# Last layer's first product as seven block products instead of eight, in a fused attention and two-layer kernel on one Trainium2 core

## Chip, core and metric

One NeuronCore of one Trainium2 chip runs the whole program. The metric is device microseconds for one execution, lower is better. All matrix products are done in fp32r with each operand split into a high and a low part, three matmuls (high·high, high·low, low·high) for each product.

## What is computed

```python
attn_out = _attn_ref(q, k, v, s)              # 4 x 8 heads x 576 tokens x 64, causal, decay bias
x = attn_out.transpose(0, 2, 1, 3).reshape(2304, 512)
a, b = x @ w_a, x @ w_b                       # 512 -> 1536, twice
y = (a * b) @ w_out                           # 1536 -> 512
h = y @ w_in2                                 # 512 -> 2048: the last layer's first product
g = np.maximum(h, 0.0) ** 2
out = g @ w_out2                              # 2048 -> 512: the last layer's second product
```

The weights come as 64-bit floats and are decoded on the chip to fp32 (helper `decode`), then split into high and low.

## The kernel before

A planner (`Plan`) takes every operation in program order with a stream ("first", "att", "moe", "next", "late"), a cost and the buffers it needs, and lists the instructions of each engine in one static order: the earliest start by its own cost figures, and among those that can start, the lowest rank (`Plan.RANK`, then program order). A DMA is issued on SP only, and SP's order is part of that list, so a DMA whose wait is not over holds up every DMA behind it. All instructions are recorded at line 246, so the profile is read by tile names.

The work, in order of time: attention of the four batches with the middle layer's chunks (`moe1`, tiles `ab`, `py`) interleaved; after the attention's pools are closed (`swap`, about 460 us) only the middle layer's last chunks of 448 tokens run; from about 723 us the last layer.

The middle layer keeps the high parts of its weights in 36 buffers "wh" and fetches the low parts for every chunk from DRAM (`lo<-wlab`, 512 KB; `loo<-wlo`, 384 KB). TensorE (PE) accumulates into three PSUM banks of the pool "mm" (`mm_bank`).

The last layer before: `split2(f)` decodes for each of the 16 blocks of 128 hidden features a block of w_in2 and one of w_out2 into `w2h`, `w2l`, kept in SBUF in buffers that the middle layer frees (tag "wh", stream "late"). The loop over `t0` takes 512 tokens at a time (four and a half times); `load_y` brings their four 128-row blocks of y from DRAM and splits them (`yhy`/`yly` or `xhy`/`xly`, double-buffered). For each f, 12 matmuls of 512 columns fill one bank `ph` (4 blocks of the contraction, 3 passes); ScalarE (ACT) and VectorE (DVE) form relu(h)² and its split, `g2h`/`g2l`; `second(f)` of the f before adds 4 × 3 matmuls of 512 columns into the four banks `po`, which are evicted and stored after the last f:

```python
for d in range(ND):
    h_, l_ = yy(d, 0, n)
    pairs += [(w2h[f, 0][:, d, :], h_), (w2h[f, 0][:, d, :], l_), (w2l[f, 0][:, d, :], h_)]
matmul(ps, n, pairs)
...
if prev is not None:
    second(*prev)
```

Of the kernel before, what the change touches and what calls it, by code (L numbers as in the profile page):

```python
# [7 lines left out]
F32 = mybir.dt.float32  # L8
F32R = mybir.dt.float32r
# [239 lines left out]
def attention_moe_moe(tc, q, k, v, s, w_a, w_b, w_out, w_in2, w_out2, out):  # L249
# [14 lines left out]
    NT1 = 2  # L264
    CC = 448
    W = 512
    NLATE = 11
    EARLY = 10
    AHEAD = 6
    LAG = 0.0  # L270
    LF = 5
    MORE = 12
# [25 lines left out]
    def gated(name, shape, dtype, tag, bufs, nm):  # L298
        return pl.tile(pool(name), shape, dtype, tag, bufs, nm, swapped)
# [11 lines left out]
        return pl.tile(pool("mm"), [P, 512], F32, "mm", 3, name)  # L311


    def pe(cost, calls, out, ins):
        pl.add({"PE": (cost, calls, False)}, [out], ins)

    def matmul(out, n, pairs, passes=1.0):
        calls = [
            ("matmul", (out, a, b), {"start": i == 0, "stop": i == len(pairs) - 1}) for i, (a, b) in enumerate(pairs)
        ]  # L320
        cost = len(pairs) * (passes * max(n, 256 if passes == 1 else n) / 2.4 + 13)
        pe(cost, calls, out, [x for pair in pairs for x in pair])
# [389 lines left out]
    def attention(b):  # L712
# [30 lines left out]
            unit(p)  # L743
        return steps

    def new_x(nm, second=False):
        if second:
            ts = [gated("lop", [P, ND, W], F32R, t, 1, f"{t}{nm}") for t in ("yh", "yl")]
# [10 lines left out]
        subtract(n, xl, xl.bitcast(F32), xh.bitcast(F32))  # L759


    def decode(w, by_col, f, hi, lo, nm, raw, t, takes, by):
# [7 lines left out]
        dma(raw.rearrange("p (d c) -> p d c", d=ND), src, 512, takes)  # L770
        words = raw.rearrange("p (n w) -> p n w", w=2)
        low, high = words[:, :, 0], words[:, :, 1]
        hi, lo = (x.rearrange("p d c -> p (d c)") for x in (hi, lo))
# [12 lines left out]
        gps("tensor_tensor", n, out=t, in0=t, in1=low, op=ALU.add)  # L786
        copy(n, hi, t.bitcast(F32), by="A")
        subtract(n, lo, t.bitcast(F32), hi.bitcast(F32), by=by)

# [7 lines left out]
    def split_w(f):  # L797
        def g():
# [5 lines left out]
            for i, w in enumerate((w_a, w_b, w_out)):  # L804
                hi = sb([P, ND, P], F32R, "wh", 3 * NF1, f"wh{f}_{i}")
                if i < 2:
                    lo = ab[:, i].part(i) if ab else spare(i)
                else:
                    lo = spare(i) if f < LF1 else sb([P, ND, P], F32R, "lo1", 1, f"wlo{f}")
                k_ = 3 * f + i  # L810
                t = ts[k_ % 2]
                if f < 9:
                    t = sb([P, DM], I32, "wh", 3 * NF1, f"wt{f}_{i}") if i == 2 else ts[i]
                words = [*raws, *more] if k_ < MORE else raws
                decode(w, i < 2, f, hi, lo, f"w{f}_{i}", words[k_ % len(words)], t, (), "PD")
# [139 lines left out]
    pl.stream = "moe"  # L955


    w2h, w2l = {}, {}
    spare = []

    def split2(f):
        for i in range(2):
            hi = sb([P, ND, P], F32R, "wh", 3 * NF1, f"w2h{f}_{i}")
            n = 2 * NF2 - 2 * f - i
            if n > NLATE:
                lo = gated("lop", [P, ND, P], F32R, "w2l", 2 * NF2 - NLATE, f"w2l{f}_{i}")
            elif n > 4:
                wide, tag, bufs = {
                    5: (W, "gh", GB), 6: (W, "gl", GB), 7: (2 * GRP * P, "loo", 2), 8: (2 * GRP * P, "loo", 2),
                    9: (DM, "lo1", 1), 10: (W, f"y{ND - 1}", 1),  # L970
                    11: (W, f"y{ND - 2}", 1),
                }[n]
                lo = sb([P, wide], F32R, tag, bufs, f"w2l{f}_{i}")[:, :DM].rearrange("p (d c) -> p d c", c=P)
            else:
                if n % 2 == 0:
                    spare.append(sb([P, 2, ND, P], F32R, "lo", 3, f"w2l{f}"))
                lo = spare[-1][:, i].part(i)
            nm = f"v{f}_{i}"
            raw = gated("lop", [P, 2 * DM], I32, "tmp", 3, f"{nm}r")
            t = sb([P, DM], I32, "wh", 3 * NF1, f"{nm}t")  # L980
            decode(w_in2 if i == 0 else w_out2, i == 0, f, hi, lo, nm, raw, t, (t, hi, lo), "P")
            w2h[f, i], w2l[f, i] = hi, lo

    y_tokens = {}

    def load_y(t0):
        n = min(512, NT - t0)
        yy = y_tokens[t0] = new_x(f"y{t0}", t0 % 1024 == 0)
        for d in range(ND):
            pieces = []  # L990
            for c, (g0, g1) in enumerate(spans):
                l, r = max(t0, g0), min(t0 + n, g1)
                if l < r:
                    pieces.append((l - t0, r - l, yd[c][d][:, l - g0 : r - g0].part(d)))
            split_x(yy, d, 0, n, pieces)

    load_y(0)
    pl.stream = "late"
    for f in range(EARLY):
        split2(f)  # L1000
    pl.stream = "moe"
    for t0 in range(0, NT, 512):
        n = min(512, NT - t0)
        yy = y_tokens.pop(t0)
        nt = n // P
        po = [gated("po", [P, 512], F32, "po", 4, f"po{t0}_{i}") for i in range(nt)]
        prev = None

        def second(f, gh, gl):
            wo, wl = (t[f, 1].rearrange("p d c -> p (d c)") for t in (w2h, w2l))  # L1010
            for i in range(nt):
                at_ = slice(i * P, i * P + P)
                calls = [
                    ("matmul", (po[i], a[:, at_], w), {"start": f == 0 and z == 0, "stop": f == NF2 - 1 and z == 2})
                    for z, (a, w) in enumerate(((gh, wo), (gh, wl), (gl, wo)))
                ]
                pe(3 * 216, calls, po[i], [gh, gl, wo, wl])

        for f in range(NF2):
            if f == AHEAD and t0 + 512 < NT:  # L1020
                load_y(t0 + 512)
            ps = mm_bank(f"ph{t0}_{f}")[:, :n]
            pairs = []
            for d in range(ND):
                h_, l_ = yy(d, 0, n)
                pairs += [(w2h[f, 0][:, d, :], h_), (w2h[f, 0][:, d, :], l_), (w2l[f, 0][:, d, :], h_)]
            matmul(ps, n, pairs)
            r = sb([P, 512], F32, "a", 2, f"r{t0}_{f}")[:, :n]
            act("activation", n, r, ps, AF.Relu, psum=True)
            dve("scalar_tensor_tensor", n, ps, ps, 0.0, r, op0=ALU.max, op1=ALU.mult)  # L1030
            gh = sb([P, W], F32R, "gh", GB, f"g2h{t0}_{f}")
            gl = sb([P, W], F32R, "gl", GB, f"g2l{t0}_{f}")
            act("copy", n, gh[:, :n], ps, psum=True)
            dve("tensor_tensor", n, out=gl[:, :n], in0=ps, in1=gh[:, :n].bitcast(F32), op=ALU.subtract)
# [5 lines left out]
            prev = (f, gh, gl)  # L1040
            if t0 == 0 and f < NF2 - EARLY:
                pl.stream = "late"
                split2(EARLY + f)
                pl.stream = "moe"
        second(*prev)
        for i in range(nt):
# [42 lines left out]
```

## Time and profile before

| | |
|---|---|
| time, median of 3 runs | 1128.77 us (1125.85 to 1129.11) |
| profiled execution, first to last instruction (span) | 1128.5 us; no other time of that execution is recorded |
| PE (matmul) busy | 1099.6 us, 97% |
| DVE, ACT, POOL busy | 625.6, 482.9, 318.4 us |
| DMA | 132.10 MB, mean 117 GB/s; HBM read 99.54 MB, written 22.69 MB |
| granted TensorE clock | 1.0 from 300 us to 1100 us |

The granted clock 1.0 is the higher of TensorE's two levels, 2.4 GHz. A row of a timeline gives start, duration, engine, operation and tile; matmuls overlap, so what one costs is the distance between starts. A row of the chain of waits merges matmuls of one tile that follow each other.

### The profile page before, as it was taken

The page shows a single profiled execution, that of the slowest core. Times are in us where ns is not written, and L with a number is a line of the kernel's source. Part 1 is how long each engine was busy: PE and PEld are TensorE (multiplying, and loading weights), DVE is VectorE, ACT ScalarE, POOL GpSimd, SP SyncE. Part 2 cuts the span into 40 slices and gives each one's busy share as a digit, 9 for nine tenths or more (in the row PEclk, how much of TensorE's full clock was granted, in tenths as well). Part 3 has the DMA queues.
Part 4 walks back from the last instruction along what each step waited for, and adds up shares of the span by engine and source line. Part 5 has one row for each costly group of instructions (what it writes and reads, how often), then busy time and mean ns, then how long its engine had stood idle before and what let it go on. Part 6 is the DMA issues. An engine that isn't in the chain of part 4 may idle for free.

```text
span 1128.5 us, 15440 instructions
## 1 busy us (share of the span) xinstructions
PE 1099.6 (97%) x5488; PEld 928.5 (82%) x5488; DVE 625.6 (55%) x1174; ACT 482.9 (43%) x1121; POOL 318.4 (28%) x274
## 2 busy tenths in 40 slices
PE   5998999999999999999999999999999999999998
PEld 3665777778899999899999999888888888888887
DVE  5776797878777777723222358987232232232232
ACT  4545686667666665421121244445232222232222
POOL 2434655655433333200100147766010010000000
PEclk9977899999999999999999999999999999999999
DMA  6433467666544443443433677642110010010010
GB/s 206 153 110 105 142 194 229 187 207 194 151 148 130 135 143 103 143 147 116 164 108 116 186 246 234 195 147 75 38 38 1 21 54 1 1 57 1 1 38 19
DMA packets 83692, 132.10 MB, mean 117 GB/s; under 512 B 9104, under 2 KB 53648, under 8 KB 83616
## 3 DMA queue, kind: packets, MB, share of 16 engines
q1 hardware_dynamic: 83616, 131.12, 37.1%
q8 instruction: 43, 0.70, 0.3%
q14 instruction: 33, 0.27, 0.1%
HBM read 99.54 MB, written 22.69 MB: 108 GB/s over the span
## 4 chain that ended last, share of the span: by engine, by line
PE 90%; DVE 6%; DMA 2%; issue 1%; SPq 0%; ACT 0%; POOL 0%; DVEq 0%; ACTq 0%; POOLq 0%
PE ab L246 24%; PE ph L246 17%; PE po L246 17%; PE py L246 12%; PE av L246 7%; PE st L246 7%; PE pt L246 5%; DVE e L246 1%; DMA roomxh<-in_moe_w_a 1%; SPq L246 0%; DVE neg L246 0%; DMA v_0r<-in_moe_w_in 0%; DVE v_1t L246 0%; DMA v_1r<-in_moe_w_out 0%; DVE v_0t L246 0%
## 5 line engine op out<-in xcount | busy, mean ns | idle before, releaser
L246 DVE SCALAR_TENSOR_TENSOR ph<-ph,r 128x512 f32<-128x512 f32 (+1 forms) x80 | 51.6, 645 | 195.0 <-ACT r L246 195.0
L246 ACT ACTIVATE r<-ph 128x512 f32<-128x512 f32 (+1 forms) x80 | 44.5, 556 | 212.5 <-PE ph L246 212.5
L246 PE MATMUL po<-w2h,g2h 128*128 128x512 f32 x288 | 112.4, 390 | 0.0
L246 PE MATMUL po<-w2h,g2l 128*128 128x512 f32 x288 | 112.3, 390 | 0.0
L246 PE MATMUL po<-w2l,g2h 128*128 128x512 f32 x288 | 112.3, 390 | 0.0
L246 ACT ACTIVATE e<-st,neg 128x192 f32<-128x192 f32 (+2 forms) x192 | 91.1, 479 | 46.8 <-DVE neg L246 42.9
L246 PE MATMUL ab<-xh,wh 128*128 128x448 f32 x288 | 106.3, 369 | 0.0
L246 PE MATMUL ab<-xh,lo 128*128 128x448 f32 x288 | 105.3, 365 | 0.0
L246 PE MATMUL ab<-xl,wh 128*128 128x448 f32 x288 | 105.2, 365 | 0.0
L246 DVE TENSOR_TENSOR ab<-ab,a 128x448 f32<-128x448 f32 (+1 forms) x60 | 38.6, 644 | 105.1 <-PE ab L246 102.5
L246 PE MATMUL pt<-ident,e 128*128 128x128 f32 (+2 forms) x480 | 86.0, 290 | 10.9 <-DVE e L246 9.0
L246 DVE TENSOR_REDUCE neg<-st 128x1 f32<-128x192 f32 (+2 forms) x192 | 77.6, 425 | 27.9 <-PE st L246 19.8
L246 PE MATMUL py<-gh,wh 128*128 128x448 f32 (+1 forms) x240 | 90.8, 379 | 0.5 <-DVE gl L246 0.5
L246 PE MATMUL py<-gh,loo 128*128 128x448 f32 (+1 forms) x240 | 89.0, 371 | 0.0
L246 PE MATMUL py<-gl,wh 128*128 128x448 f32 (+1 forms) x240 | 88.9, 370 | 0.0
L246 PEld LDWEIGHTS pt<-ident,e 128*128 128x128 f32 (+2 forms) x480 | 55.7, 138 | 37.2 <-issue 11.7
L246 PE MATMUL av<-ph,val 128*128 128x256 f32 (+3 forms) x256 | 81.5, 409 | 3.1 <-DVE ph L246 1.4
L246 DVE TENSOR_TENSOR g2l<-ph,g2h 128x512 fp32r<-128x512 f32 (+1 forms) x80 | 51.0, 637 | 41.8 <-ACT g2h L246 37.2
L246 ACT COPY a<-ab 128x448 f32<-128x448 f32 (+1 forms) x60 | 32.6, 544 | 91.6 <-PE ab L246 91.5
L246 PE MATMUL ph<-yhy,w2h 128*128 128x512 f32 (+1 forms) x192 | 67.9, 354 | 0.4 <-DVE gl L246 0.4
L246 PE MATMUL ph<-yhy,w2l 128*128 128x512 f32 (+1 forms) x192 | 67.9, 354 | 0.0
L246 PE MATMUL ph<-yly,w2h 128*128 128x512 f32 (+1 forms) x192 | 67.9, 354 | 0.0
(205 smaller groups left out, 2640.2 us busy)
## 6 DMA issues: line engine op xcount, KB each, us to landing
lo<-wlab SPq DMA_DIRECT2D x48, 512.0 KB
loo<-wlo SPq DMA_DIRECT2D x40, 384.0 KB
v_0r<-in_moe_w_in SPq DMA_DIRECT2D x16, 512.0 KB
v_1r<-in_moe_w_out SPq DMA_DIRECT2D x16, 512.0 KB
roomxh<-in_moe_w_a SPq DMA_DIRECT2D x10, 512.0 KB
roomxh<-in_moe_w_b SPq DMA_DIRECT2D x10, 512.0 KB
roomxl<-in_moe_w_out SPq DMA_DIRECT2D x9, 512.0 KB
out<-o SPq DMA_DIRECT2D x18, 256.0 KB
```

Of the source, the lines that this page charges most:

```text
L246: getattr(eng, method)(*map(real, args), **{k: real(a) for k, a in kw.items()})
```

## The change

The 2 × 2 block form of Strassen's product (Winograd's variant, seven products). A pair `j` of feature blocks (f = 2j, 2j+1) is the one dimension of two, the upper and lower 256 of the 512 contraction rows the second, and two neighbouring groups of 384 tokens the third. Tokens go in sets of 768 (three sets).

- `split_in(j)` (stream "late", before `load_y(0)`) decodes the two blocks of w_in2, forms the four sums of weight blocks (`combine`), splits seven blocks of 128 × 256 into high and low (`w2h`, `w2l`, 1792 columns each) and writes both to DRAM (`w2q`, 917,504 bytes each).
- For each pair and token set two DMAs bring these back (`w`, tag "wq", 4 buffers, so two pairs).
- `load_y(t0)` brings four blocks of 128 × 768, forms four sums in place and splits seven blocks (`b11`, `b22`, `b21`, `t1` to `t4`, each high and low: 14 buffers "yq", all in use by one token set).
- A pair is seven products of 6 matmuls of 384 columns. Products with `start=False` add to a bank that ACT has already read: bank a takes b11, then t2, t3, t4; a second bank b21; a third t1, then b22. Such a product has to wait for the ACT copy (`kept`: s1, s2, s3) or the DVE sum (`relu2`) that reads the bank.
- `second(j, g)` takes both feature blocks and six token groups: 6 × 6 matmuls of 512 columns. The sixth `po` bank is one of the three "mm" banks.
- w_out2 is decoded as before (`split_out`, 16 blocks kept in SBUF).

```diff
+    def split_in(j):
+        t = temp(I32, f"w2t{j}")
+        ts = [t[:, i * DM : i * DM + DM].part(i) for i in range(2)]
         for i in range(2):
...
+            words(w_in2, True, 2 * j + i, temp(I32, f"w2r{j}_{i}"), ts[i])
+        f0, f1 = (x.bitcast(F32) for x in ts)
+        a11, a12, a21, a22 = f0[:, :QW], f0[:, QW:], f1[:, :QW], f1[:, QW:]
+        hi, lo = block(f"w2h{j}"), block(f"w2l{j}")
...
+        split(0, 2, 0, f0)
+        split(2, 3, 1, a22)
+        combine(QW, a22, a21, a22, ALU.add)
+        combine(QW, a21, a11, a21)
+        combine(QW, a11, a22, a11)
+        combine(QW, a12, a12, a11)
+        split(3, 7, 2, t.bitcast(F32))
+        for z, x in enumerate((hi, lo)):
+            dma(w2q[j][z], x.rearrange("p q c -> p (q c)").bitcast(F32), 1200)
...
+        for j in range(PAIRS):
+            nm = f"{t0}_{j}"
+            w = [block(f"w{nm}_{z}") for z in range(2)]
+            for z in range(2):
+                dma(w[z].rearrange("p q c -> p (q c)").bitcast(F32), w2q[j][z], 896)
+
+            def product(ps, q, x, start=True):
+                xh, xl = yq[x]
+                pairs = []
+                for d in range(2):
+                    wh_, wl_ = (z[:, q, d * P : d * P + P] for z in w)
+                    pairs += [(wh_, xh[:, d]), (wh_, xl[:, d]), (wl_, xh[:, d])]
+                matmul(ps, CW, pairs, start, 0.0 if start else STEP)
...
+            def relu2(m, n, ps, s):
...
+                if s is None:
+                    act("activation", CW, v, ps, AF.Relu, psum=True)
+                    dve("tensor_tensor", CW, out=v, in0=v, in1=v, op=ALU.mult, two=True)
+                else:
+                    dve("tensor_tensor", CW, out=v, in0=ps, in1=s, op=ALU.add)
+                    dve("scalar_tensor_tensor", CW, v, v, 0.0, v, op0=ALU.max, op1=ALU.mult, two=True)
+                copy(CW, gh, v, by="A")
+                subtract(CW, gl, v, gh.bitcast(F32), by="D")
+
+            a = mm_bank(f"pa{nm}")[:, :CW]
+            product(a, 0, "b11")
+            s1 = kept("a", 2, 512, 1, a)
+            b = mm_bank(f"pb{nm}")[:, :CW]
+            product(b, 1, "b21")
+            relu2(0, 0, b, s1)
+            product(a, 3, "t2", False)
+            s2 = kept("lo1", 1, DM, 2, a)
+            b = mm_bank(f"pc{nm}")[:, :CW]
+            product(b, 6, "t1")
+            product(a, 5, "t3", False)
+            s3 = kept("a", 2, 512, 3, a)
+            relu2(1, 1, b, s3)
+            product(a, 2, "t4", False)
+            relu2(1, 0, a, None)
+            product(b, 4, "b22", False)
+            relu2(0, 1, b, s2)
             if prev is not None:
                 second(*prev)
...
+            prev = (j, g)
+        if t0 + 2 * CW < NT:
+            load_y(t0 + 2 * CW)
         second(*prev)
```

How the planner lists the work now is shown at three places.

PE in the last layer, middle of a token set. Before, the end of one feature block's 12 matmuls (`ph`, 512 columns) and the start of `second` of the block before (`po`):

```order
L246 MATMUL ph_9_7875<-yhy_6588,w2h_0_7465 128x512
L246 MATMUL ph_9_7875<-yly_6551,w2h_0_7465 128x512
L246 MATMUL ph_9_7875<-yhy_6588,w2l_0_7470 128x512
L246 MATMUL po_0_7513<-w2h_1_7423,g2h_8_7871 128x512
L246 MATMUL po_0_7513<-w2l_1_7427,g2h_8_7871 128x512
L246 MATMUL po_0_7513<-w2h_1_7423,g2l_8_7890 128x512
```

Now, in pair 3 (`pa` is bank a, `po_2` a group of 6 matmuls of `second` of pair 2):

```order
L246 MATMUL pa_3_8006<-t3h_7072,w_3_0_7828 128x384
L246 MATMUL pa_3_8006<-t3l_7092,w_3_0_7828 128x384
L246 MATMUL pa_3_8006<-t3h_7072,w_3_1_7832 128x384
L246 MATMUL po_2_7787<-w2o_0_7423,gxh_2_7905 128x512
L246 MATMUL po_2_7787<-w2o_1_7438,gxh_2_7905 128x512
L246 MATMUL po_2_7787<-w2o_0_7423,gxl_2_7918 128x512
L246 MATMUL po_2_7787<-w2o_0_7457,gxh_2_7905 128x512
L246 MATMUL po_2_7787<-w2o_1_7470,gxh_2_7905 128x512
L246 MATMUL po_2_7787<-w2o_0_7457,gxl_2_7918 128x512
L246 MATMUL pa_3_8006<-t4h_7123,w_3_0_7828 128x384
L246 MATMUL pa_3_8006<-t4l_7139,w_3_0_7828 128x384
L246 MATMUL pa_3_8006<-t4h_7123,w_3_1_7832 128x384
```

Between t3 and t4, which add to the same bank with an ACT copy in between, now stands one group of six `po` matmuls. A whole pair lists: b11, b21, po, t2, t1, po, t3, po, t4, b22, po, po, po.

PE at the start of the second and of the third token set (tokens 768 and 1536), first pair:

```order
L246 MATMUL pa_1_8757<-b11h_8523,w_1_0_8626 128x384
L246 MATMUL pa_1_8757<-b11l_8525,w_1_0_8626 128x384
L246 MATMUL pa_1_8757<-b11h_8523,w_1_1_8630 128x384
L246 MATMUL pa_0_8713<-t3h_8568,w_0_0_8484 128x384
L246 MATMUL pa_0_8713<-t3l_8589,w_0_0_8484 128x384
L246 MATMUL pa_0_8713<-t3h_8568,w_0_1_8489 128x384
L246 MATMUL pa_0_8713<-t3h_8568,w_0_0_8484 128x384
L246 MATMUL pa_0_8713<-t3l_8589,w_0_0_8484 128x384
L246 MATMUL pa_0_8713<-t3h_8568,w_0_1_8489 128x384
L246 MATMUL pa_0_8713<-t4h_8678,w_0_0_8484 128x384
L246 MATMUL pa_0_8713<-t4l_8691,w_0_0_8484 128x384
L246 MATMUL pa_0_8713<-t4h_8678,w_0_1_8489 128x384
```

Here no `po` work is left to stand between t3 and t4; only pair 1's first product was moved ahead of t3.

SP, the queue that issues all DMAs. Before, no weight of the last layer (`v`) is read until the middle layer's last chunk, where the list runs:

```order
L246 DMA yly_6551<-yd_3123 128x512 x4
L246 DMA lo_3_6586<-wlab_1072 128x1024
L246 DMA v_0r<-in_moe_w_in 128x4x256
L246 DMA yd_6612<-y_0_0_0_6134 128x448
L246 DMA loo_0_0_6625<-wlo_523 128x768
L246 DMA yd_6612<-y_0_0_1_6146 128x448
```

Now the reads of w_in2 (`w2r`) and the writes of the split blocks (`w2q`) begin more than a chunk earlier, and at this place, in the last-but-one chunk, they stand among the middle layer's loads:

```order
L246 DMA w2q_0_6145<-w2h_5947 128x1792
L246 DMA lo_4_6181<-wlab_1240 128x1024
L246 DMA w2q_1_6200<-w2l_5987 128x1792
L246 DMA lo_5_6218<-wlab_1494 128x1024
L246 DMA w2r_0_6237<-in_moe_w_in 128x4x256
L246 DMA lo_6_6250<-wlab_1770 128x1024
L246 DMA loo_1_0_6280<-wlo_1231 128x768
L246 DMA w2r_1_6282<-in_moe_w_in 128x4x256
```

A `w2q` write waits for ACT or for DVE and POOL to finish its block, and the `lo` behind it waits with it.

## Rows read from the trace of the kernel before

**Rows 1.** The page, busy time by engine, and the chain of waits by engine.

```profile
PE 1099.6 (97%) x5488; PEld 928.5 (82%) x5488; DVE 625.6 (55%) x1174; ACT 482.9 (43%) x1121; POOL 318.4 (28%) x274
...
PE 90%; DVE 6%; DMA 2%; issue 1%; SPq 0%; ACT 0%; POOL 0%; DVEq 0%; ACTq 0%; POOLq 0%
```

**Rows 2.** Windows of all engines: stretch, its length, busy us (instructions) by engine, clock, DMA share, GB/s.

```profile
640.00:660.00 20.00, 20.00 (x100) 18.54 (x99) 10.33 (x19) 7.22 (x13) 6.15 (x5) 1.00 0.83 257
...
680.00:700.00 20.00, 20.00 (x101) 18.53 (x100) 15.50 (x21) 9.74 (x18) 14.17 (x11) 1.00 0.76 261
700.00:720.00 20.00, 19.51 (x97) 17.76 (x96) 18.38 (x25) 7.81 (x15) 13.97 (x11) 1.00 0.59 186
720.00:740.00 20.00, 19.62 (x92) 16.78 (x91) 19.59 (x27) 9.10 (x17) 12.85 (x9) 1.00 0.62 198
820.00:860.00 40.00, 40.00 (x179) 33.10 (x178) 12.17 (x18) 9.99 (x18) 3.54 (x3) 1.00 0.07 27
```

**Rows 3.** Groups of instructions with their shapes kept apart, PE: count, busy us, mean ns.

```profile
L246 PE MATMUL po<-w2h,g2h 128*128 128x512 f32 x288 | 112.4, 390 | 0.0
...
L246 PE MATMUL ph<-yhy,w2h 128*128 128x512 f32 x128 | 49.9, 390 | 0.4 <-DVE gl L246 0.4
...
L246 PE MATMUL ph<-yhy,w2h 128*128 128x256 f32 x64 | 18.0, 282 | 0.0
```

**Rows 4.** Chain of waits from 600 us on: start, length, what, matmuls.

```profile
646.59 14.59 PE ab L246 x72
...
837.26 2.72 PE ph L246 x12
839.98 2.72 PE po L246 x12
```

**Rows 5.** Timeline of PE, a run of 12 matmuls of 256 columns: first, and what follows the last.

```profile
1076.45 0.28 PE L246 MATMUL ph<-yhy,w2h 128*128 128x256 f32 x1
...
1077.89 0.40 PE L246 MATMUL po<-w2h,g2h 128*128 128x512 f32 x1
```

**Rows 6.** Timeline of PE, a matmul of 320 columns and the next start.

```profile
443.71 0.31 PE L246 MATMUL av<-ph,vs 128*128 128x320 f32 x1
443.86 0.60 PE L246 MATMUL pt<-ident,e 128*128 128x128 f32 x4
```

**Rows 7.** Timeline of PE, the start that follows a full ph bank.

```profile
845.25 0.39 PE L246 MATMUL po<-w2h,g2h 128*128 128x512 f32 x1
```

**Rows 8.** Timeline of ACT, what reads that bank, and the last split before the end.

```profile
845.51 0.60 ACT L246 ACTIVATE r<-ph 128x512 f32<-128x512 f32 x1 [3.49 <-PE ph L246]
...
1122.69 0.37 ACT L246 CAST g2h<-ph 128x256 fp32r<-128x256 f32 x1 [0.50 <-DVE ph L246]
1124.82 0.59 ACT L246 COPY o<-po 128x512 f32<-128x512 f32 x1 [1.75 <-PE po L246]
```

**Rows 9.** Timeline of PE, the first matmul that uses that split.

```profile
1123.12 0.50 PE L246 MATMUL po<-w2h,g2h 128*128 128x512 f32 x1
```

**Rows 10.** Groups by shape, ACT and DVE, evictions of 384 columns.

```profile
L246 ACT COPY ph<-pt 128x384 f32<-128x384 f32 x14 | 6.7, 479 | 10.7 <-PE av L246 5.9 <-PE pt L246 4.7
...
L246 DVE COPY ph<-pt 128x384 f32<-128x384 f32 x18 | 9.9, 551 | 3.2 <-PE av L246 1.7 <-PE pt L246 1.3
```

**Rows 11.** Timeline of SP: issues at the two ends of the stretch.

```profile
490.71 1.74 SPq L246 DMA_DIRECT2D yl<-xd  x4
...
664.86 3.97 SPq L246 DMA_DIRECT2D loo<-wlo  x2
```

**Rows 12.** One tile of the decoding, ns minimum/median/maximum.

```profile
L246 DVE SCALAR_TENSOR_TENSOR v_1t<-v_1r,v_1t x16: 674/680/1691, 658.3 to 783.0; 128x512 int32<-128x512 int32 x16
L246 POOL TENSOR_TENSOR v_1t<-v_1t,v_1r x16: 1310/1424/1502, 659.4 to 786.1; 128x512 int32<-128x512 int32 x16
```

**Rows 13.** Waits of PE from 640 to 745 us: total, times, longest.

```profile
PE py L246 <- DVE gl L246: 0.5, 1, 0.5
PE ph L246 <- DVE gl L246: 0.4, 1, 0.4
```

More of the change, by code (lines that the diff above doesn't have):

```diff
@@ L311, in mm_bank, with pe, matmul @@
         return pl.tile(pool("mm"), [P, 512], F32, "mm", 3, name)
-    def pe(cost, calls, out, ins):
-        pl.add({"PE": (cost, calls, False)}, [out], ins)
-    def matmul(out, n, pairs, passes=1.0):
+    def pe(cost, calls, out, ins, lag=0.0):
+        pl.add({"PE": (cost, calls, False)}, [out], ins, lag=lag)
+    def matmul(out, n, pairs, start=True, lag=0.0):
+        more = {} if start else {"skip_group_check": True}
         calls = [
-            ("matmul", (out, a, b), {"start": i == 0, "stop": i == len(pairs) - 1}) for i, (a, b) in enumerate(pairs)
-        ]
-        cost = len(pairs) * (passes * max(n, 256 if passes == 1 else n) / 2.4 + 13)
-        pe(cost, calls, out, [x for pair in pairs for x in pair])
+            ("matmul", (out, a, b), {"start": start and i == 0, "stop": i == len(pairs) - 1, **more})
+            for i, (a, b) in enumerate(pairs)
+        ]
+        cost = len(pairs) * (n / 2.4 + 13)
+        pe(cost, calls, out, [x for pair in pairs for x in pair], lag)
     def on_dve(method, n, *args, two=False, each=1.04, **kw):
@@ L744, in attention, with quad @@
         return steps
+    def quad(nm):
+        return gated("lop", [P, 2 * CW], F32R, "yq", 14, nm)
     def new_x(nm, second=False):
         if second:
-            ts = [gated("lop", [P, ND, W], F32R, t, 1, f"{t}{nm}") for t in ("yh", "yl")]
+            ts = [[quad(f"x{nm}_{z}_{d}") for d in range(ND)] for z in range(2)]
+            return lambda d, o, n: [t[d][:, o : o + n] for t in ts]
         else:
@@ L769, in decode @@
             src = w[f * P : f * P + P, :].rearrange("p (d c) -> p d c", d=ND)
[L770 to L773, printed above, removed]
+        dma(raw.rearrange("p (d c) -> p d c", d=ND), src, 700 if pl.stream == "late" else 512, takes)
+        pairs = raw.rearrange("p (n w) -> p n w", w=2)
+        low, high = pairs[:, :, 0], pairs[:, :, 1]
         hf = high.bitcast(F32)
@@ L786, in decode @@
         gps("tensor_tensor", n, out=t, in0=t, in1=low, op=ALU.add)
+    def decode(w, by_col, f, hi, lo, raw, t, takes, by):
+        words(w, by_col, f, raw, t, takes)
+        n = ND * P
+        hi, lo = (x.rearrange("p d c -> p (d c)") for x in (hi, lo))
         copy(n, hi, t.bitcast(F32), by="A")
@@ L955, in attention_moe_moe @@
     pl.stream = "moe"
-    w2h, w2l = {}, {}
-    spare = []
-    def split2(f):
-        for i in range(2):
[L963 to L982, printed above, removed]
@@ L984, in attention_moe_moe @@
-    y_tokens = {}
-    def load_y(t0):
[L987 to L995, printed above, removed]
+    PAIRS = NF2 // 2
+    QW = 2 * P
+    w2q = [[scratch([P, 7 * QW], F32, f"w2q{j}_{z}") for z in range(2)] for j in range(PAIRS)]
@@ new lines, in attention_moe_moe, with split_out, pull, split @@
+    w2o = {}
+    def split_out(f):
+        hi, lo = (sb([P, ND, P], F32R, "wh", 3 * NF1, f"w2o{f}_{z}") for z in range(2))
+        raw = temp(I32, f"w2or{f}")
+        t = temp(I32, f"w2ot{f}")[:, :DM]
+        decode(w_out2, False, f, hi, lo, raw, t, (t, hi, lo), "PD")
+        w2o[f] = [x.rearrange("p d c -> p (d c)") for x in (hi, lo)]
+    y_quads = {}
+    def load_y(t0):
+        def pull(x, k, n0, nm):
+            for d in range(2):
+                a = t0 + n0 * CW
+                for c, (g0, g1) in enumerate(spans):
+                    l, r = max(a, g0), min(a + CW, g1)
+                    if l < r:
+                        dma(
+                            x[:, d * CW + l - a : d * CW + r - a],
+                            yd[c][2 * k + d][:, l - g0 : r - g0].part(2 * k + d), (r - l) * 0.5,
+                        )
+            return x
+        n = 2 * CW
+        b11, b12, b22, b21 = (
+            pull(temp(F32, f"yr{t0}_{k}{h}")[:, :n], k, h, f"{t0}_{k}{h}") for k, h in ((0, 0), (0, 1), (1, 1), (1, 0))
+        )
+        lo, hi = {}, {}
+        def split(x, v):
+            lo[x], hi[x] = quad(f"{x}l{t0}"), quad(f"{x}h{t0}")
+            copy(n, hi[x], v)
+            subtract(n, lo[x], v, hi[x].bitcast(F32))
+        split("b11", b11)
+        split("b22", b22)
+        combine(n, b22, b22, b12)
+        split("b21", b21)
+        combine(n, b12, b12, b11)
+        split("t3", b22)
+        combine(n, b11, b11, b22, ALU.add)
+        split("t1", b12)
+        combine(n, b21, b21, b11)
+        split("t2", b11)
+        split("t4", b21)
+        y_quads[t0] = {
+            x: [t[x].rearrange("p (d c) -> p d c", d=2) for t in (hi, lo)] for x in hi
+        }
@@ L997, in attention_moe_moe @@
+    pl.stream = "late"
+    for j in range(PAIRS):
+        split_in(j)
+    pl.stream = "moe"
     load_y(0)
     pl.stream = "late"
-    for f in range(EARLY):
-        split2(f)
+    for f in range(NF2):
+        split_out(f)
     pl.stream = "moe"
[L1002 to L1006, printed above, removed]
-        prev = None
[L1009 to L1034, printed above, removed]
@@ L1039, in attention_moe_moe @@
                 tail.clear()
[L1040 to L1044, printed above, removed]
+            prev = (j, g)
+        if t0 + 2 * CW < NT:
+            load_y(t0 + 2 * CW)
         second(*prev)
-        for i in range(nt):
+        for i in range(6):
             o = sb([P, W], F32, f"y{i % 2}", 1, f"o{t0}_{i}")[:, :DM]
```

57 lines of the change are left out of this document (50 added, 7 removed).

## The prediction

> **What bounds the kernel now.** I read the page first. PE is busy for 97% of the span, and 90% of the chain that ended last is PE work [rows 1]; so PE is the engine to look at, and the other four matter only where PE waits for them. The windows then tell whether that holds in the stages that the change touches. In the last layer a window of 40 us has PE busy for 40.00, DVE for 12 and DMA at a share of 0.07 [rows 2]: here the time is the number of matmuls times the distance between their starts, nothing else. While the middle layer's last chunks run, PE is also full, and DVE and DMA are far busier (DVE 19.59 of 20.00, DMA share 0.83); between 700 and 740 us PE loses 0.5 and 0.4 us to DVE, which is behind with decoding [rows 2, 13]. So PE work taken away in the last layer comes off the end, as long as no new wait takes its place, and work that is added to the other engines is free until PE waits for it.
>
> **First product, the gain.** Removed are 768 matmuls of 512 columns (two tile names, three passes, 128 each) and 192 of 256 [rows 3]. A run of 12 of 512 takes 2.72 us, 0.2267 each [rows 4]; 12 of 256 take 1077.89 − 1076.45 = 1.44 us, 0.120 each [rows 5]. Together 174.1 + 23.0 = 197.1 us. Added are 3 token sets × 8 pairs × 7 products × 6 = 1008 matmuls of 384 columns, against 1152 if eight products were made. No row has that width. Columns at 2.4 GHz plus a fixed part describe the others: 512 and 256 carry 13.3 ns; 320 takes 0.15 us, 133.3 + 16.7 ns [rows 6]; 448 takes 14.59/72 = 0.2026, 186.7 + 15.9 ns [rows 4]. So 384 costs 173.3 to 176.7 ns. Of its neighbours one is of each kind, so I take the middle, 175: 176.4 us in all (174.7 to 178.1). **Gain 20.7 us (19.0 to 22.4).**
>
> The Trainium skill, in "TensorE: Matmul & The Clock Gate", section "Wait — 56ns, not 53.3ns?", states for warm bf16 matmuls the columns at 2.4 GHz plus about 2.5 ns; by it the gain would be an estimated 22.9 us. The 13.3 ns in this trace do not agree with it, and the measurement decides.
>
> **Second product.** 288 × 3 = 864 matmuls of 512 before [rows 3], 3 × 8 × 36 = 864 after. Zero.
>
> **Inside a pair.** A pair is 42 × 0.175 + 36 × 0.2267 = 15.5 us of PE. Beside it run 8 ACT and 11 DVE instructions of 384 columns, at 479 and 551 ns [rows 10]: 3.8 and 6.1 us. Neither engine becomes the bound. The new thing is that a product adds to a bank that has just been read. ACT starts 845.51 − 845.25 = 0.26 us after the start that follows a full bank [rows 7, 8]; the copy takes 0.48; PE starts 1123.12 − 1123.06 = 0.06 after ACT's end [rows 8, 9]. So t4 can start 0.80 us after t3. The list has six `po` matmuls between them, 1.36 us: a margin of 0.56. The DVE sum that frees the third bank for b22 comes 0.6 us after the copy, with `po` and t4 (2.4 us) as cover. t2 and t3 have more. Zero for 24 pairs, and 0.80 each where that cover is gone.
>
> **Starts of the second and third token set.** There it is gone: t3 and t4 stand back to back, 2 × 0.80 = 1.6 us. Six `po` banks are now evicted through two buffers, so the third eviction of a buffer waits for the second's store; at the end a store takes from 1125.41, where the last eviction ends [rows 8], to 1128.5, 3.1 us. The sixth bank is one of three "mm" banks, and pair 1's first product, moved ahead, wants it 4.2 us after the last `po`. That is about one eviction and one store, with y loads between the stores on SP at the second set. Bounds: nothing, or a further store at both starts (6.2); I take 2, nearer to nothing, since the lengths just fit. The 14 "yq" buffers are single: the next set's seven splits and four sums (7 copies on ACT at twice 479 ns, 11 sums and subtractions at twice 551: 18.8 us) and pair 7's own 9.9 us have to fit between pair 7's first product and the new set, 36 × 0.175 + 66 × 0.2267 = 21.3 us. 28.7 us of work on three engines at once fits, so I count zero. **Loss 3.6 us (1.6 to 7.8).**
>
> **Preparing the weights.** The 16 blocks of w_in2 are now decoded, summed, split and written to DRAM under the middle layer's last two and a half chunks, and w_out2's 16 after that. DVE and POOL get this work earlier and spread wider, which is good for the 0.9 us lost today [rows 13]. What is new is traffic. From SP's position of the x load at 490.7 us to that of the `loo` pair at 664.9 to 668.8 [rows 11] the list now holds 50.7 MB (16 × 0.52 w2r, 16 × 0.92 w2q written, 4 × 0.92 read back, the middle layer's own 24 × 0.52 + 16 × 0.39, and 5 of x and y); before, 25.3. That is 286 GB/s for 178 us. Windows of today reach 257 and 261 GB/s at shares of 0.83 and 0.76 with PE at 20.00 of 20.00 [rows 2], which puts a full share at 310 to 343: the load fits, at 83 to 92%. Behind a w2q write that waits for ACT or POOL on SP stands an `lo` load, and PE waits for that; an `lo` is issued two feature blocks (2 × 24 × 0.2026 = 9.7 us [rows 4]) ahead. I take 1.5 us (−0.9, if today's loss goes and none comes, to 6). **Loss 1.5 us.**
>
> **Reading them back.** 1.835 MB per pair of 15.5 us is 118 GB/s, and a load is issued a pair ahead; even at the 198 GB/s of 720 to 740 us [rows 2] it takes 9.3 us. Zero. The end (last split, six `po` groups, eviction, store) stays as it is.
>
> **Sum.** 1128.5 − 20.7 + 3.6 + 1.5 = 1112.9 on the profiled span; the median of the runs stands 0.3 above that span. **1113 us.**
>
> **Rivals.**
> *Handoffs inside the pairs.* ACT takes its work in order; a cast that waits for DVE may stand ahead of s3. Once s3 is over 0.56 us late, every pair pays. For it: one `po` group is all the cover. Against: ACT has 3.8 us of work in 15.5. Half a microsecond in each of 24 pairs gives 1125, the whole 0.80 gives 1132. Chance 0.09.
> *DMA becomes the bound before 723 us, and the kernel slower.* The place is the stretch above, the price its length: 50.7 MB at 225 GB/s, the mean of the four windows shown from 640 to 740 us [rows 2], take 225 us, 47 more, hence near 1159. It decides below 50.7 MB/(178 + 17) = 260 GB/s, where the 17 us of net gain are eaten. For it: no window of today is above 261. Against: PE waited for no transfer in those windows, so they show what was asked, not what can be had. Chance 0.06.
> *POOL holds up DVE.* The slowest of 16 DVE instructions on a decoded block took 1691 ns against a median of 680, so one was held about 1.0 us, beside POOL instructions of 1424 [rows 12]. Three of the new 1024-column subtractions are listed on POOL, some 2.8 us each. If a DVE eviction is held for the whole of each and PE waits, 8.4 us: 1121. Against: in the window with DVE at 15.50 and POOL at 14.17 of 20 us PE did not wait at all [rows 2]. Chance 0.06. The Trainium skill, "SBUF — State Buffer", section "Who interferes with whom", says that a DVE instruction with two SBUF inputs and a GpSimd instruction that reads SBUF exclude each other for the whole instruction; that maximum agrees, though this row alone does not show who held whom.
> *The change does not do what it says.* The list has the 1008 matmuls, so 0.01.
>
> **How the numbers follow.** The forecast's own range is 1128.8 − 22.4 + 1.6 − 0.9 = 1107 to 1128.8 − 19.0 + 7.8 + 6 = 1124; it gets the remaining 0.78. The range given, 1106 to 1124, has a microsecond more below, since the 0.80 rests on handoffs after other shapes; it takes in POOL's case and the mildest of the handoffs, about 0.86. No change is within 0.3%, 3.4 us, about what a measurement can tell: 1125.4 to 1132.2. Faster: 0.78 + 0.06 + half of the handoffs = 0.89. Same: the other half and the last rival, 0.05. Slower: DMA, 0.06.
>
> **What would show it.** Right: 1008 matmuls of 384 columns, six in about 1.05 us of the chain; windows inside a token set with PE full; two short PE waits, 0.8 us for ACT and one for a bank, at the starts of sets two and three. Wrong: a repeated wait of PE for ACT between t3 and t4 (handoffs), idle PE before `ab` for `lo` from DMA between 490 and 723 us (traffic), a pitch of 384 outside 173 to 177 ns, or waits for `w`.

## The result and the profile after

The changed kernel takes **1107.9 us** (median of four runs, 1106.7 to 1108.7) against 1127.3 us for the kernel before beside it. The ratio is 0.9836, with a 95% interval of 0.9801 to 0.9871, so 18.5 us (14.5 to 22.4) are gone. The forecast was 1113, that is 15.8 less.

| | before | after |
|---|---|---|
| profiled execution: its own time, us | not recorded | 1106.7 |
| span, us | 1128.5 | 1104.9 |
| first matmul of the last layer, us | 723.1 | 717.6 |
| from there to the end, us | 405.4 | 387.4 |
| PE instructions | 5488 | 5536 |
| DMA, MB in the span, mean GB/s | 132.10, 117 | 190.86, 173 |

In both kernels 36 `py` matmuls of the middle layer still stand behind that first matmul, so the fourth line compares like with like: the last layer is 18.0 us shorter. The 48 more PE instructions are the 1008 matmuls of 384 columns in place of 960. The other 5.6 us of the difference between the two spans lie ahead of the last layer, and the run of the kernel before further down shows that all but 1.3 of them do not belong to the change.

The page, busy time by engine and the chain by engine, which answer to [rows 1]:

```profile
PE 1075.8 (97%) x5536; PEld 935.0 (85%) x5536; DVE 687.9 (62%) x1326; ACT 509.3 (46%) x1176; POOL 305.2 (28%) x265
...
PE 93%; DVE 4%; DMA 1%; ACT 1%; issue 1%; SPq 0%; POOL 0%; DVEq 0%; ACTq 0%; POOLq 0%
```

PE still sets the time. DVE has 62 us more work than before, and its share of the chain fell from 6% to 4%.

Windows of the changed kernel, columns as in [rows 2]:

```profile
490.00:560.00 70.00, 70.00 (x347) 64.89 (x346) 46.70 (x76) 27.97 (x49) 24.96 (x20) 1.00 0.85 287
...
640.00:660.00 20.00, 20.00 (x100) 18.54 (x99) 5.02 (x8) 4.42 (x8) 0.00 (x0) 1.00 0.95 321
...
720.00:740.00 20.00, 20.00 (x106) 18.93 (x106) 15.77 (x28) 9.33 (x19) 7.13 (x5) 1.00 0.66 232
820.00:860.00 40.00, 39.43 (x198) 35.32 (x197) 25.54 (x38) 14.95 (x28) 7.65 (x4) 1.00 0.49 171
```

The traffic of the preparation is there (287 GB/s over 70 us, 321 over 20 us), and PE is busy for every microsecond of it. The stretch from 720 to 740 us, which lost 0.4 us before, is full. The last window holds the start of the second token set and is short of 0.57 us.

The waits of PE from 440 us to the end, as the profile lists them (total, times, longest):

```profile
PE pa L246 <- ACT s L246: 1.1, 2, 0.6
PE av L246 <- DVE pl L246: 0.4, 1, 0.4
```

The two waits for ACT are the starts of the second and third set. There is none for a bank, for a store, for `w`, for `lo` or for a quad (one of the 14 buffers "yq" with the sums of y). The list leaves out the shortest waits; those show only in the distance between starts. Both waits of [rows 13] are gone (in the two later profiles of this kernel one `py` wait of 0.4 us for DVE is left).

One pair in the chain of waits, from its first product to the next pair's:

```profile
779.48 1.06 PE pa L246 x6
780.54 1.04 PE pb L246 x6
781.58 1.39 PE po L246 x6
782.97 1.04 PE pa L246 x6
784.01 1.04 PE pc L246 x6
785.05 1.39 PE po L246 x6
786.44 1.04 PE pa L246 x6
787.49 1.39 PE po L246 x6
788.88 1.04 PE pa L246 x6
789.92 1.04 PE pc L246 x6
790.96 4.12 PE po L246 x18
795.08 1.06 PE pa L246 x6
```

The pair takes 15.60 us and nothing but PE work is in it. Two durations are to be read here. Six matmuls of 384 columns take 1.04 us, 0.1733 each, at the lower end of what was forecast. Six `po` matmuls that stand alone take 1.39 us, 0.2317 each, and 18 in a row take 4.12, 0.2289, while the kernel before made twelve in 2.72, 0.2267 each [rows 4]. So a pair's share of the second product, which the prediction counted as unchanged, takes 1.39 × 3 + 4.12 = 8.29 us instead of 36 × 0.2267 = 8.16. Either run of `po`, of 6 or of 18, takes 0.03 to 0.04 us more than 0.2267 for each of its matmuls. The trace of the kernel before has such runs too, where `ph` is 256 columns wide; one of them in its chain:

```profile
1082.23 1.39 PE po L246 x6
```

### The profile page after: what moved, and what is told of

Read it like the earlier page. It is cut to its first block, busy times and chain, and to the rows that moved or that the text cites. A ratio compares the mean times of both kernels' runs of the same rounds, so it can differ in the third digit from the quotient of the medians.

```text
span 1104.9 us, 15776 instructions
## 1 busy us (share of the span) xinstructions
PE 1075.8 (97%) x5536; PEld 935.0 (85%) x5536; DVE 687.9 (62%) x1326; ACT 509.3 (46%) x1176; POOL 305.2 (28%) x265
## 2 busy tenths in 40 slices
DMA packets 94063, 190.86 MB, mean 173 GB/s; under 512 B 10256, under 2 KB 56336, under 8 KB 93984
## 4 chain that ended last, share of the span: by engine, by line
PE 93%; DVE 4%; DMA 1%; ACT 1%; issue 1%; SPq 0%; POOL 0%; DVEq 0%; ACTq 0%; POOLq 0%
PE ab L246 26%; PE po L246 18%; PE py L246 13%; PE pa L246 9%; PE av L246 7%; PE st L246 7%; PE pt L246 6%; PE pc L246 5%; PE pb L246 2%; DVE e L246 1%; DVE neg L246 1%; SPq L246 0%; DVE ph L246 0%; DMA raw_0q<-in_q 0%; DVE roomxl L246 0%
## 5 line engine op out<-in xcount | busy, mean ns | idle before, releaser
L246 PE MATMUL ab<-x,wh 128*128 128x512 f32 (+1 forms) x384 | 117.5, 387 | 0.0
L246 ACT COPY s<-pa 128x384 f32<-128x384 f32 x72 | 34.3, 480 | 145.8 <-PE pa L246 145.6
L246 PE MATMUL po<-w2o,gxh 128*128 128x512 f32 x288 | 89.3, 391 | 0.0
L246 PE MATMUL po<-w2o,gh 128*128 128x512 f32 x288 | 89.2, 391 | 0.0
L246 PEld LDWEIGHTS ab<-x,wh 128*128 128x128 f32 x384 | 72.0, 191 | 9.9 <-issue 0.3
L246 DVE TENSOR_TENSOR v<-pc,s 128x384 f32<-128x384 f32 x48 | 26.5, 553 | 70.4 <-ACT s L246 70.4
L246 ACT CAST gh<-ab 128x448 fp32r<-128x448 f32 (+1 forms) x60 | 32.5, 542 | 67.6 <-DVE ab L246 67.5
L246 ACT COPY a<-ab 128x448 f32<-128x448 f32 (+1 forms) x60 | 32.5, 542 | 66.7 <-PE ab L246 66.5
L246 PEld LDWEIGHTS po<-w2o,gh 128*128 128x128 f32 x288 | 53.5, 188 | 9.2
L246 PEld LDWEIGHTS po<-w2o,gxh 128*128 128x128 f32 x288 | 53.4, 188 | 8.6
```

Of the source, the lines that this page charges most:

```text
L246: getattr(eng, method)(*map(real, args), **{k: real(a) for k, a in kw.items()})
```

## The experiments

The last layer is given as the time from its first matmul to the end of the profiled span, from unrounded times. In three profiles of the changed kernel (the one above and two later ones) it is 387.4, 388.1 and 388.0 us; in two of the kernel before 405.4 and 405.4. A ratio is to the kernel before, run beside the variant on the same chip, with its 95% interval. The groups of runs were on different chips, so a variant's effect is read from its last layer first.

### An eighth product

```diff
             product(a, 0, "b11")
+            product(a, 0, "b11")
```

> The changed kernel with an eighth block product: in every pair the first product (b11) is computed a second time into the same bank, 24 x 6 more matmuls of 384 columns, nothing else added. Theory (the last layer's time is the number of matmuls times their pitch): 144 x 0.1735 us, the pitch that the changed kernel's trace shows, = +25.0 us, so 1107.9 + 25.0 = 1132.9 us, slower than the kernel before (1127.3) by about 5.6. Rival (a part of the gain came from waits that the change took away elsewhere, and the seven products are partly hidden behind something else): clearly less than +25, 1115 to 1125.

Measured: 1133.25 us median (ratio to before 1.0078, 1.0049 to 1.0107), last layer 413.2 us. The chain of a pair begins:

```profile
783.37 1.06 PE pa L246 x6
784.43 1.04 PE pb L246 x6
785.47 1.04 PE pa L246 x6
786.51 1.39 PE po L246 x6
...
800.01 1.06 PE pa L246 x6
```

The third line is the product that was added, and the pair takes 16.64 us instead of 15.60. That is +25.4 us by the medians and +25.1 to 25.8 in the last layer, as the theory has it; PE waits for `s` three times instead of twice, and that is 0.9 of it. A product more costs all of its PE time, so one that is left out is worth as much. With eight products, the new order by itself would lose: the change pays only through the one product in eight that Strassen's scheme saves.

### Without the cover between t3 and t4

```diff
-                pe(6 * 227, calls, po[i], ins)
+                pe(6 * 227, calls, po[i], [*ins, *last] if i > 1 else ins)
...
-                second(*prev)
+                second(*prev, [a])
```

`last` names t4's bank to the planner, so that four of the six `po` groups are listed behind t4.

> The changed kernel with the group of six po matmuls taken out from between t3 and t4 in every pair that has one (21 of 24) and put behind b22; no instruction is added or removed. Theory (t4 can start 0.80 us after t3's last matmul, the copy of the bank on ACT being 0.48 of it): 21 x 0.80 = +16.8 us, so about 1124.7 us, and a PE wait for ACT 21 times more, about 0.55 each as the profile counts it (as at the two starts of sets). Rival (the handoff is hidden by the matmuls queued on PE, or is shorter within a set): +0 to +5 us. Rival of the other side (ACT is behind there, so that the handoff takes longer than 0.80): above +20 us.

Measured: 1122.6 us (ratio 0.9963, 0.9937 to 0.9988), 14.8 above the changed kernel's 1107.9, last layer 402.9 us, 15.5 longer. PE waits for `s` on ACT 20 times instead of twice, 12.3 us in all. The timelines of PE and of ACT at one of these places, the last matmul of t3 and the first two of t4:

```profile
789.71 0.34 PE L246 MATMUL pa<-t3h,w 128*128 128x384 f32 x1
790.67 0.44 PE L246 MATMUL pa<-t4h,w 128*128 128x384 f32 x1 [0.62 <-ACT s L246]
790.95 0.34 PE L246 MATMUL pa<-t4l,w 128*128 128x384 f32 x1
```

```profile
790.14 0.48 ACT L246 COPY s<-pa 128x384 f32<-128x384 f32 x1 [3.00 <-PE pa L246]
```

The mechanism holds, and the price is a little higher. With no wait, t4 would start 0.17 us after t3's last matmul, at 789.88. The copy starts 0.26 us after that and takes 0.48, and t4 starts 0.05 after its end: 0.79 us, against the 0.80 of the prediction. What the prediction left out comes behind: t4's second matmul starts 0.28 us after its first instead of 0.17. That makes 0.90 us for one uncovered handoff. The number of places was miscounted: the list made 18 of them, not 21, since in the second pair of each set a `po` group stayed where it was. 18 × 0.90 = 16.2 us; the `po` groups, now in fewer runs, give 0.5 back.

### The prepared blocks written twice

```diff
             dma(w2q[j][z], x.rearrange("p q c -> p (q c)").bitcast(F32), 1200)
+            dma(twice[j][z], x.rearrange("p q c -> p (q c)").bitcast(F32), 1200)
```

> The changed kernel with each prepared pair of weight blocks written to DRAM twice, the second time to a place that nobody reads: 14.7 MB more in the same stretch (about 490 to 668 us), 65.4 MB instead of 50.7. Theory (a full share of the DMA engines is about 338 GB/s, worked out from 321 GB/s at a share of 0.95): 65.4 MB need 193 us, 15 more than the stretch has, so PE begins to wait for the lo loads, and since the preparation can run on into the last layer for the later pairs, a part is absorbed: +5 to +15 us, with PE waits for DMA between 550 and 720 us. Rival (the writes stand behind loads on SP and fill gaps only): +0 to +2 us and the prepared blocks later.

Measured: 1124.2 us (ratio 0.9987, 0.9954 to 1.0021), 16.3 above the changed kernel, last layer 403.8 us. The size is just above the theory's, and the place is another, so neither theory nor rival holds. From 490 to 720 us PE has one wait, of 0.3 us for DVE, and none for `lo`. PE, in the timeline, stops two matmuls into the last layer:

```profile
720.72 0.33 PE L246 MATMUL pa<-b11l,w 128*128 128x384 f32 x1
731.05 1.01 PE L246 MATMUL pa<-b11h,w 128*128 128x384 f32 x2 [10.00 <-DMA w<-w2q]
```

SP, in the timeline, shows why: the second half of the first pair's `w` is issued at 722.77 us, behind the writes of later pairs.

```profile
719.36 0.49 SPq L246 DMA_DIRECT2D w2q<-w2h  x1
719.89 0.43 SPq L246 DMA_DIRECT2D tw<-w2h  x1
720.37 2.00 SPq L246 DMA_DIRECT2D yr<-yd  x2
722.77 0.81 SPq L246 DMA_DIRECT2D w<-w2q  x1
```

In the changed kernel that load, the second of `w`, is issued at 641.56 us, 76 us ahead of the first matmul:

```profile
641.56 0.61 SPq L246 DMA_DIRECT2D w<-w2q  x1
```

So the preparation has some 76 us to spare, and what runs out when it gets heavier is this reserve, not the `lo` loads. Of the 16.4 us that the last layer is longer, this wait is 10.0. Two more waits, 1.6 and 0.2 us, are for a late quad, t1, and PE waits for `s` three times instead of twice, which is 0.9 us. The remaining 3.7 us lie between 731 and 741 us, where PE, after it had stood still, ran at the lower level of the clock.

```profile
724.00:726.00 2.00, 0.00 (x0) 0.00 (x0) 0.00 (x0) 0.00 (x0) 0.00 (x0) 0.50 1.01 416
738.00:740.00 2.00, 2.00 (x8) 1.88 (x7) 2.00 (x3) 1.28 (x2) 0.00 (x0) 0.50 0.98 385
740.00:742.00 2.00, 2.00 (x12) 1.90 (x11) 1.10 (x3) 0.00 (x0) 0.00 (x0) 0.97 0.83 264
```

The granted clock is 0.50, 1.2 GHz, while PE stands still and up to 740 us, after PE was busy again: 8 matmuls in 2 us instead of 12.

### The kernel before, once more

> The kernel before, once more, for its profile. Theory (of the 23.6 us between the two profiled spans some 4 us arise before 140 us, where both kernels have the same instructions, and come from a stretch in which TensorE was granted its lower clock longer in that one execution): in this profile the first matmul of the last layer starts somewhere between 717 and 725 us, by how long the lower clock was granted between 75 and 135 us, and the last layer itself again takes 405.4 us from its first matmul. Rival (the 4 us belong to the kernel before): again 723 us and again three stretches at half clock of about 7, 17 and 7 us.

Measured: 1126.75 us, span 1125.0, first matmul of the last layer at 719.6 us, last layer 405.4 us. The rival falls. The changed kernel varies in the same way: in its other profiles, and in those of its variants, the last layer begins between 712.3 and 722.4 us. The windows from 50 to 100 us of the kernel before, of the changed kernel, and of the second run of the changed kernel (last layer from 712.3 us):

```profile
50.00:100.00 50.00, 45.04 (x179) 29.18 (x178) 36.02 (x80) 24.91 (x72) 18.19 (x17) 0.76 0.30 98
```

```profile
50.00:100.00 50.00, 43.19 (x185) 28.60 (x186) 39.88 (x86) 26.34 (x76) 21.47 (x19) 0.80 0.36 112
```

```profile
50.00:100.00 50.00, 43.57 (x200) 29.10 (x201) 41.72 (x91) 28.16 (x83) 26.21 (x22) 0.87 0.44 137
```

A higher granted clock goes with more matmuls in the same 50 us (179, 185, 200) and an earlier last layer. This is before any instruction that the change touches: PE's list is the same in both kernels up to far behind this place, and its 450th matmul starts at 133.7 and 128.9 us in the two profiles of the kernel before, at 129.9 and 123.7 in the two of the changed kernel. Whole runs go the same way: in the six of the changed kernel to which the last of these profiles belongs, a mean granted clock of 0.991 or 0.992 goes with 1102.1 to 1102.9 us, 0.986 with 1108.7 and 1108.9, 0.983 with 1111.5. So the spread of some 10 us between runs of one program goes with this clock, and the effect of the change is better read from the last layer than from two spans.

One stretch ahead of the last layer does belong to the change. From PE's 3300th matmul (at 655.1 and 650.9 us in the first profile of either kernel) to the last layer's first, 328 matmuls take 68.0 us in both profiles of the kernel before and 66.7 in all three of the changed kernel: what the waits of [rows 13] had cost.

### All po groups in one block (recorded as e2_block)

```diff
-                pe(6 * 227, calls, po[i], ins)
+                pe(6 * 227, calls, po[i], [*ins, *last])
...
-                second(*prev)
+                second(*prev, [b])
```

> The changed kernel with all six po groups of a pair behind the next pair's first product, so that the other six products of a pair stand together (t2, b21, t3, t1, t4, b22) and 36 po matmuls stand together; at the starts of sets a product of the next pair stands between t3 and t4. No instruction is added or removed. Theory (a handoff to ACT takes 0.80 us and one over DVE about 0.87; each is covered by one product of 1.04 us, and a matmul of 512 in a group of six that stands alone costs 0.2315 against 0.2275 in a long run): no waits inside the pairs, the two waits of 0.55 at the starts of sets gone, and about 2 us off the second product: 1104 to 1106 us. Rival (DVE and ACT take their work in order, and 11 DVE instructions of 551 ns now fall into 7.3 us, so that a sum that frees a bank comes late): a PE wait of 0.2 to 0.5 us in most pairs, 1110 to 1118.

Measured: 1121.2 us (ratio 0.9942, 0.992 to 0.9964), last layer 398.8 us, a pair 16.00 us. The rival holds, in a form that the list of waits hardly shows. The `po` block is as cheap as expected, but the other six products take more than it gives:

```profile
780.43 1.06 PE pa L246 x6
...
788.23 8.20 PE po L246 x36
796.43 1.06 PE pa L246 x6
```

ACT, in the timeline, shows what held `s`: the cast ahead of it on ACT's list had waited 1.69 us for DVE.

```profile
783.76 0.51 ACT L246 CAST gxh<-v 128x384 fp32r<-128x384 f32 x1 [1.69 <-DVE v L246]
784.18 0.47 ACT L246 COPY s<-pa 128x384 f32<-128x384 f32 x1
```

PE, in the timeline, shows what t4 (from 784.70) lost by it:

```profile
784.28 0.34 PE L246 MATMUL pc<-t1h,w 128*128 128x384 f32 x1
784.70 0.44 PE L246 MATMUL pa<-t4h,w 128*128 128x384 f32 x1
784.98 0.34 PE L246 MATMUL pa<-t4l,w 128*128 128x384 f32 x1
```

t4 starts 0.42 us after the matmul ahead of it instead of 0.17, and its second matmul 0.28 after its first: 0.36 us in all. This is the prediction's rival "handoffs inside the pairs", in the form it was given there. It is about half of the 11 us. Most of the rest are 8 long waits for `s`, 5.3 us in the list, at places in the first pairs of the sets where this list, too, leaves two products on bank a back to back. Whether ACT's order or DVE's load was to blame is left open by this run, and the next one settles it.

### The same block, with the copy ahead of the cast

```diff
-                copy(CW, gh, v, by="A")
+                act("copy", CW, gh, v, lag=1000.0)
```

`act` passes the lag on to the planner, which then lists s3 ahead of that cast. The order on PE inside the sets stays; on DVE the sum that frees b22's bank moves ahead of a subtraction.

> The order of e2_block once more, with one thing changed: on ACT the copy s3 of a bank stands ahead of the cast that waits for DVE, in every pair; PE's order is that of e2_block. Theory (e2_block lost 0.4 us a pair because ACT takes its work in order: the cast waited for DVE ahead of s3, t4 waited for s3, and PE then needs 0.25 us to fill again): the pair goes from 16.00 us to 15.4 or 15.5, the last layer from 398.8 us to 385 to 387, as long as or shorter than the changed kernel's 387.2. Rival (it is DVE that is behind, with 11 instructions in 7.3 us, and the order on ACT does not matter): the last layer stays within 2 us of 398.8.

Measured: 1113.4 us (ratio 0.9894, 0.9858 to 0.993), last layer 391.8 us, 7.1 less than before this edit. Inside the sets the pair is at 15.52 us, with no wait:

```profile
779.46 8.20 PE po L246 x36
787.66 1.06 PE pa L246 x6
...
794.98 5.03 PE po L246 x22
```

```profile
790.90 0.48 ACT L246 COPY s<-pa 128x384 f32<-128x384 f32 x1 [1.60 <-PE pa L246]
791.28 0.52 ACT L246 CAST gxh<-v 128x384 fp32r<-128x384 f32 x1
```

Here s starts as soon as t3 is done and t4 waits for nothing, while DVE has the same 11 instructions. So the order on ACT was the cause, and DVE's load was not. The Trainium skill, in "Perfetto Trace Analysis", section "Tensor Engine Instruction (MATMUL, LD_WEIGHTS)", says that ACT, DVE and GpSimd take their work strictly in order, and the two timelines of ACT agree with that. The total missed its range, since this list, like the one before it, leaves two products on bank a back to back in the first pairs of the sets: PE waits for `s` 8 times, 4.8 us in all. Six more than in the changed kernel, at 0.90, are 5.4 us, and 391.8 − 5.4 = 386.4 is where the theory put it.

### No delay for the adding products

```diff
-    STEP = 600.0
+    STEP = 0.0
```

> The changed kernel with the planner's delay of 600 ns on the adding products set to 0: of the three po groups that stand alone in a pair only the one between t3 and t4 stays, the other five stand together; t2 is covered by one product of 1.04 us and t3 by one too. Theory (handoff 0.80 us; a switch from 384 to 512 columns costs some 26 ns, and two fewer are made in each of 21 pairs): no new PE wait, 1 us less, 1106 to 1108. Rival (the covers were needed, since ACT is not always free): PE waits for ACT before t2 or t3, +2 to +8.

Measured: 1106.9 us (ratio 0.984, 0.9805 to 0.9875), beside 1105.8 for the changed kernel on the same chip; last layer 387.1 us, and no new wait in the list. One `po` run of 30 takes 6.84 us, 0.228 each, so the 36 `po` matmuls of a pair take 8.23 us instead of 8.29. By the starts in the timeline all `po` work of the last layer is 1.2 us shorter, as the theory has it, and one of the two waits at the starts of sets is gone, 0.85 more. But the seven products took 1.7 us longer elsewhere, in waits too short for the list (in three pairs b22 starts some 0.27 us late), so the last layer is 0.3 us shorter than the shortest of the changed kernel. The covers are nearly, not quite, unneeded, and the times cannot tell the two kernels apart.

### All splits of the prepared weights on POOL

```diff
-            subtract((r - l) * QW, o, src, h.bitcast(F32))
+            subtract((r - l) * QW, o, src, h.bitcast(F32), by="P")
```

> The changed kernel with every subtraction that splits the prepared weights put on POOL: 8 of 1024 columns instead of 3, 8 of 512 instead of 4, 8 of 256 instead of 1, which DVE did otherwise. Theory (the preparation has some 50 us to spare before its first use, and DVE is half idle in that stretch): no PE wait before the last layer, 1107 to 1109 us. Rival (a POOL instruction of 2.46 us holds a DVE instruction with two inputs for its whole length, and an eviction of the middle layer behind it makes PE wait): PE waits for DVE between 490 and 720 us, up to 8 x 2.46 = 20 us, at a third of that 1114.

Measured: 1104.5 us (ratio 0.9806, 0.9774 to 0.9837), last layer 387.4 us, no wait of PE between 490 and 720 us:

```profile
490.00:560.00 70.00, 70.00 (x347) 64.86 (x346) 43.04 (x64) 25.49 (x45) 41.78 (x34) 1.00 0.83 282
```

POOL is busy for 41.78 us here instead of 24.96, and PE for all 70.

### The changed kernel, twice more

> The changed kernel once more, on the chip of the runs beside it. Theory: 1107.9 us as before, the last layer 387.2 us from its first matmul, its first matmul at 717.0 to 718.5 us. Rival (the 4 us that the two profiles of before differ by ahead of 140 us also come in the changed kernel): a first matmul at 720 us or later.

> The changed kernel beside it on the same chip, for the difference in time to the run beside it: 1102 to 1111 us, by how long TensorE is granted its lower clock before 140 us, and 387 to 388 us from the first matmul of the last layer. Rival: a last layer that itself varies by more than 2 us between executions.

Measured: 1105.8 us (ratio 0.9819, 0.9787 to 0.9852) and 1107.1 us (ratio 0.9837, 0.9807 to 0.9866); last layers 388.1 and 388.0 us, starting at 712.3 and 717.9. The last layer repeats within 0.7 us (the `py` wait of 0.4 us that the first profile lacks, and the slow matmul behind it), its start does not: the first theory was wrong to expect a fixed start. No variant beats the changed kernel by what can be measured; the inside of a pair at 15.52 with the covers kept at the starts of the sets would be worth at most 24 × 0.08 = 1.9 us, an estimate, and was not made.

## Why the prediction was right, point by point

Its forecast, faster by the PE work that goes, is what happened, and the eighth product shows that this is the cause. The terms, in us (plus is longer); what is shown is summed over the starts in the first profiles of both kernels:

| term | forecast | shown |
|---|---|---|
| first product | −20.7 | −21.2 |
| second product | 0 | +1.5 |
| handoffs inside a pair | 0 | 0 |
| starts of sets 2 and 3 | +3.6 | +1.7 |
| preparing the weights | +1.5 | −1.3 |
| reading them back, the end | 0 | 0 |
| sum | −15.6 | −19.3 |

- **First product.** 960 matmuls took 197.1 us, as the prediction has it; the 1008 took 177.6, of which 1.7 are the starts of the sets. A pair's 42 take 7.30 us, 0.1738 each, inside the bounds. At 384 columns the fixed part is again 13.3 ns (0.1733 us), not the 2.5 ns that the Trainium skill, "TensorE: Matmul & The Clock Gate", section "Wait — 56ns, not 53.3ns?", has for its bf16 matmuls.
- **Second product.** This term was put at zero and is not. Equal numbers of equal matmuls were counted at equal cost, at the 0.2267 of runs of twelve between `ph` of the same width. Between products of another width a run of `po` takes 0.03 to 0.04 us more, whether it has 6, 18 or 36 matmuls (8.20 instead of 8.16), so what costs is the number of runs, four a pair. The kernel before had 14 runs of six between `ph` of 256 columns, at 1.39 us, and a few others above 0.2267, so the price stood in its trace. All 864 `po` matmuls, last eviction and store included, took 200.9 us before and 202.4 after.
- **Inside a pair.** Zero, as forecast. The run without the cover shows that the 0.80 is right as far as it goes, that 0.11 more comes behind it, and that 18 covers are worth 15.5 us; the block order shows that the rival was a real one and that it hangs on one place in ACT's list.
- **Starts of the sets.** The two handoffs came, at 0.85 each. The 2 us for banks and stores did not: no such wait is in the trace, and the prediction's sign of a wait for a bank did not show.
- **Preparing the weights.** The loss was guessed at 1.5; there is none, and the two waits of [rows 13] went, which is worth 1.3. In the two later profiles a `py` wait inside the last layer takes 0.7 of that back, and the sum is −18.6. The DMA rival needed less than 260 GB/s, and the trace shows 287 and 321 with PE full. The POOL rival falls with the run that put all splits there. The Trainium skill, "SBUF — State Buffer", section "Who interferes with whom", says that two-input DVE and GpSimd reads exclude each other; whether they do or not, no run here shows a microsecond that PE lost by it.
- **The sum.** −18.6 to −19.3 from the stages stands beside −18.5 (14.5 to 22.4) from the times. The forecast of −15.8 was some 3 us too cautious: two losses that were guessed, 2 us for banks and stores and 1.5 for the preparation, did not come, and one that nobody had looked for, 1.5 us in the second product, hid a part of it. That the errors partly cancel is luck. The measured 1107.9 lies near the lower end of the range, whose upper part stood for these guesses. The 0.3 us that the forecast adds at the end set the median of some executions against the span of another; wherever both are recorded for one execution, its time is 1.7 to 1.9 us above its span.

## What to carry to other kernels

Where PE is full, a matmul taken away is worth its pitch (the distance between starts), but what surrounds it has to be listed so that other matmuls fill the 0.80 us in which a bank's reader works. Look at the order on the reader's engine too: a copy that PE waits for must not stand behind an instruction that waits for a third engine. Count 0.03 to 0.04 us for each run of matmuls between others of another width, and judge a change of this size by the stage it touches, not by two spans.

## What the runs showed of the hardware

- Six matmuls of 512 columns between others of 384 took 1.39 us, 18 took 4.12 and 36 in a block 8.20: each run 0.03 to 0.04 us above 0.2267 a matmul. The cause is not settled.
- A wait of PE costs more than the wait itself: the first matmul behind it took 0.28 us until the next start instead of 0.17 (384 columns, clock 1.0).
- The DMA engines moved 416 GB/s at a full share (1.01) in the run with twice the writes, while PE stood still, where the prediction had worked out 310 to 343.
- With the same instructions, TensorE's mean granted clock from 50 to 100 us was 0.76, 0.80 or 0.87 in different executions, and the last layer of the changed kernel and its variants started between 712.3 and 722.4 us. What sets the clock there was not tried.
